# Pooled attention: sums of four tokens made by adding transfers, under a planner that models the tensor clock

## The chip, the cores and the metric

The kernel runs on one core of one Trainium2 chip. The metric is the device time of one execution in microseconds (us); the time of the kernel before is the median of three runs.

## What is computed

```python
# q, k, v: (B=8, H=8, S=576, D=64); w1, w2, w3: (512, 768); w_out: (768, 512)
q_d = q.reshape(B, H, 144, 4, D).mean(axis=3)      # k_d, v_d alike
out_d = sm_attn(q_d, k_d, v_d)                     # softmax attention over 144 pooled tokens
out_up = np.repeat(out_d, 4, axis=2)
mask = np.abs(pos[:, None] - pos[None, :]) < 4     # seven neighbours
out_local = softmax(where(mask, scale * q @ k.T, -1e9)) @ v
x = (out_up + out_local).transpose(0, 2, 1, 3).reshape(B * S, H * D)      # (4608, 512)
h = np.maximum(np.maximum(x @ w1, x @ w2), x @ w3)
return h @ w_out
```

The MLP weights arrive as float64. The means are made as sums; their quarter is in the scale of the scores and in later factors.

## The kernel before

The work is cut into nine blocks, j = 0 to 8. Blocks 0 to 7 hold the first 512 tokens of a batch each, block 8 the last 64 of all eight. Each of the first eight has two halves of four heads, n = 2j and 2j + 1. The engines are TensorE (PE), VectorE (DVE), ScalarE (ACT), GpSimd (POOL) and SyncE (SP), which issues every DMA of this kernel.

*Local attention.* Blocks 0 and 1 are "dense" (`dense`, L1132): `band_load` (L777) brings q and k transposed, `band_scores` (L813) multiplies them on TensorE and takes the softmax of a band (row maxima `mxb`, sums `zb`, the scaling `wlo<-wlo,zb`), `band_values` (L847) multiplies with v. Blocks 2 to 7 work by windows (`scores` L706, `values` L746): products `prod` and sums on VectorE, products `pv` on GpSimd or ScalarE.

*Pooled attention* needs, for each half, the transposed sums `qkT` (128 x 2 x 2 x 144: q and k, two pairs of heads, 128 sums and 16 of the tail), the sums of v as `vd` (128 x 4 x 64) and of v's tail as `vs` (128 x 64). `pooled_scores` (L634) takes maxima `nm`, the exponentials and `pd`, `ptail`; `pooled_values` (L686) gives `od` and `odtail`. The sums come from four places. `tail_pooled` (L611) loads `traw` and `pt` and adds twice by way of `th`. In dense blocks `band_sums` (L801) adds the band's own q and k (by way of tag `q`), and `band_pooled_values` (L878) loads v again and adds it by way of `hv`. In windowed blocks `scores` loads `qt_pool` and `kt_pool` into `hqk` and adds them by way of `qd` and `kd` on GpSimd, and `values` adds the v that it has by way of `hv`.

*MLP.* `turn(j)` (L1168) transposes a block's x and splits it into two float32r parts, `xhi` and `xlo` (`xlo<-t,xhi`, one per 128 columns, four per block). A weight comes in 24 pieces of 512 KB (`weight_piece`, L583); `weight_split` (L572) makes of each a float32 (`hqk`: an absolute value on ScalarE, two TENSOR_SCALAR and two SCALAR_TENSOR_TENSOR, STT below, on VectorE) and its two parts `whi` and `wlo` (or `wo`). `mlp_column` (L912) makes 128 hidden columns with three groups of twelve matmuls, the contraction chunks c = 0 to 3 in order:

```python
ops = [(a[ft][:, i, c], b[c]) for c in range(NCC) for a, b in ((whi, blk["hi"]), (wlo, blk["hi"]), (whi, blk["lo"]))]
```

and `mlp_out` (L929) multiplies with `w_out`. The last two blocks go through `joint_in` (L1047), which shares products between them.

*What sets the order.* Every operation is first recorded (`Recorder`, L150; hence all of them show one line in the trace, L459, after the change L499). `place` (L288) then lays them on five engines by prices (`price`, L244), priorities and a model of the DMA rings (`Rings`, L116), and `emit` (L415) writes them out in that order, one queue per engine, each executed in sequence. Priorities are set with `at(...)`: `FIRST` and `LATE` for the halves of dense blocks, a line in the number of pieces for weights (L1176). TensorE's prices are multiplied by a fixed 1.65 between 11 and 82 us:

```python
if e == "PE" and WARM < t < SLOW:
    c *= COLD
```

Of the kernel before, what the change touches and what calls it, by code (L numbers as in the profile page):

```python
# [21 lines left out]
P = 128  # L22
# [22 lines left out]
WPRIO = (20.0, 60.0, 105.0, 150.0, 160.0, 170.0, 180.0)  # L45
# [62 lines left out]
def pe_kind(o):  # L108
    method, args, _ = o.forms["PE"][0]
    if method == "transpose":  # L110
        return "T" if list(args[1].ap)[0][1] > T32 else "t"
    kind = {F32R: "R", BF16: "B"}.get(args[1].dtype, "M")
    return "P" if kind == "M" and elems(args[0]) in (P, 6) else kind


class Rings:  # L116
# [6 lines left out]
    def issue(self, t, on_chip, outside):  # L123
        src, dst = [[list(d) for d in ap.ap] for ap in (outside, on_chip)]
        run = src.pop()[1] if src[-1][0] == 1 and len(src) > 1 else 1
        rows = int(np.prod([c for _, c in src]))
        k = max(x for x in range(1, 17) if src[0][1] % x == 0 and dst[0][1] % x == 0)
        each = rows // k
        lane = self.count % LANES
        self.count += 1  # L130
        t = max(t, self.lanes[lane])
        while True:
            left = sum(n * min(1.0, (b - max(t, a)) / (b - a)) for a, b, n in self.queue if b > t)
            if left + each <= RING or not left:
# [12 lines left out]
        return t, done, end  # L147


class Recorder:  # L150
# [93 lines left out]
    def price(self, eng, method, args, kw):  # L244
# [7 lines left out]
        if eng == "PE":  # L252
# [11 lines left out]
            return 165.0 if n > P else 125.0, False  # L264
# [15 lines left out]
        if eng == "POOL":  # L280
            if method == "memset":
# [6 lines left out]
    def place(self):  # L288
        ops = self.ops
        for o in ops:  # L290
            o.users, o.left, o.ready, o.eng, o.waits = [], len(o.need), 0.0, None, []
            o.cost = {}
# [15 lines left out]
        rings = Rings()  # L308
        queue = {e: [] for e in ENGINES}
# [24 lines left out]
        while len(out) < len(ops):  # L334
# [34 lines left out]
            if e == "PE" and WARM < t < SLOW:  # L369
                c *= COLD  # L370
# [5 lines left out]
            else:  # L376
# [3 lines left out]
                o.end = t + c + DONE_NS[e]  # L380
            o.stop = free[e]
# [16 lines left out]
            for u in o.users:  # L398
                u.left -= 1
                same = tuple(u.forms) == (e,) and e != "SP"  # L400
# [70 lines left out]
def local_global_attention_maxout_kernel(ctx: ExitStack, tc: tile.TileContext, q, k, v, qt_dense, kt_dense, qt_pool, kt_pool, qkt_tail, v_dense, v_tail, w_in, w_out, ident_d, mask_d, band_d, out):  # L471
# [139 lines left out]
    def tail_pooled(n):  # L611
        j, h0 = n // 2, HH * (n % 2)
        st = state[n]
        qkT = st["qkT"]
        dense_n = n < 2 * NDENSE
        raws = []
        for g, src in enumerate((qkt_tail[j, n % 2], v_tail[j, h0 : h0 + HH])):
            tag = (("traw", "pt") if n != 1 else ("traw", "k"))[g] if dense_n else "traw"
            raw = new([P, FAC * D], tag=tag, bufs=2 if tag == "k" else 1, name=f"traw_{n}_{g}")
            with late(n):  # L620
                sp.dma_start(raw, src if g == 0 else src.rearrange("h r x -> (h r) x"))
            h = new([P, 2 * D], tag="th", name=f"th_{n}_{g}")
# [83 lines left out]
    def scores(n):  # L706
# [7 lines left out]
        for g in range(HH):  # L714
# [10 lines left out]
            if j < B:  # L725
                w, pr = ("q", "k")[g // 2], g % 2
                if g == 0:
                    qkT = st["qkT"] = new([P, 2, 2, SD], tag="qkT", bufs=2, name=f"qkT_{n}")
                raw = new([P, SEG], tag="hqk", bufs=2, name=f"raw{w}_{n}_{pr}")
                sp.dma_start(raw, (qt_pool, kt_pool)[g // 2][j - NDENSE, h0 // 2 + pr])  # L730
                half = new([P, 2 * P], tag=f"{w}d", name=f"h{w}_{n}_{pr}")
                tt(half, raw[:, : 2 * P], raw[:, 2 * P :], ALU.add, ("POOL",))
                tt(qkT[:, g // 2, pr, :P], half[:, :P], half[:, P:], ALU.add)
# [12 lines left out]
    def values(n):  # L746
# [4 lines left out]
        if j < B:  # L751
            hv = new([P, HH, 2 * D], tag="hv", name=f"hv_{n}")
            vd = st["vd"] = new([P, HH, D], tag="vd", bufs=2, name=f"vd_{n}")
        for g in range(HH):
# [11 lines left out]
            if j < B:  # L766
                halves(n, "v", vv[:, 3 * D : 7 * D], hv[:, g])
# [5 lines left out]
        if j < B:  # L773
            tt(vd, hv[:, :, :D], hv[:, :, D:], ALU.add)
# [25 lines left out]

    def band_sums(n, pr, tag):  # L801
        st = state[n]
        if pr == 0:
            st["qkT"] = new([P, 2, 2, SD], tag="qkT", bufs=2, name=f"qkT_{n}")
        qkT, band = st["qkT"], st["band", pr]
        for a, x0 in enumerate((0, SEG + 3)):
            dst3 = band[:, x0 : x0 + SEG].rearrange("p (r f) -> p r f", f=FAC)
            h = new([P, P, 2], tag="q", bufs=2, name=f"hq_{n}_{pr}_{a}")
            o1 = qkT[:, a, pr, :P]
            pair = [("tensor_tensor", (), dict(out=h, in0=dst3[:, :, :2], in1=dst3[:, :, 2:], op=ALU.add)), ("tensor_tensor", (), dict(out=o1, in0=h[:, :, 0], in1=h[:, :, 1], op=ALU.add))]  # L810
            rec.add({"POOL": pair, "DVE": pair})
# [65 lines left out]

    def band_pooled_values(n):  # L878
        j, h0 = n // 2, HH * (n % 2)
        vd = state[n]["vd"] = new([P, HH, D], tag="vd", bufs=2, name=f"vd_{n}")  # L880
        hv = new([P, HH, 2 * D], tag="hv", name=f"hv_{n}")
        for g in range(0, HH, 2):
            vv = new([P, 2, FAC * D], tag="v", bufs=2, name=f"v_{n}_{g}")
            with late(n):
                sp.dma_start(vv, dram(v, (j * H + h0 + g) * S * D, [[FAC * D, P], [S * D, 2], [1, FAC * D]]))
            halves(n, "v", vv, hv[:, g : g + 2])
        tt(vd, hv[:, :, :D], hv[:, :, D:], ALU.add)

# [229 lines left out]
    def attention(n):  # L1118
        j = n // 2
        if n % 2 == 0:  # L1120
            state["blk", j] = {"x": [None] * NCC, "band": {}, "hi": [], "lo": []}
            if j == B:
                state["blk", j]["od"] = odtail.rearrange("p c b t -> p c (b t)")
        scores(n)
        if j < B:
            tail_pooled(n)
# [5 lines left out]
    def dense(j):  # L1132
# [5 lines left out]
        def pooled(n, _):  # L1138
            tail_pooled(n)
            pooled_scores(n)  # L1140
            band_pooled_values(n)
# [66 lines left out]
def lay_out(q, k, v, moe_w1, moe_w2, moe_w3, moe_w_out):  # L1208
    first, rest = slice(0, NDENSE), slice(NDENSE, B)
# [3 lines left out]
    for name, x in zip(("qt_pool", "kt_pool"), pairs):  # L1213
        named[name] = x[rest, :, :, :SEG].reshape(B - NDENSE, H // 2, P, P, FAC).swapaxes(3, 4).reshape(B - NDENSE, H // 2, P, SEG)
    tails = np.stack([x[..., SEG:].reshape(B, 2, 2, P, TAIL, FAC) for x in pairs])
    named["qkt_tail"] = tails.transpose(1, 2, 4, 0, 3, 6, 5).reshape(B, 2, P, FAC * FAC * TAIL)
    named["v_dense"] = v[first].transpose(0, 2, 1, 3).reshape(NDENSE, S, H * D)
    named["v_tail"] = v[:, :, FAC * (SD - T32) :].reshape(B, H, T32, FAC * D)
# [30 lines left out]
```

## Time and profile before

| | |
|---|---|
| median of three runs | 742.05 us (742.05, 742.05, 742.7) |
| the profiled execution: its time and its span | 742.2 us (nothing lies around the span), 11812 instructions |
| TensorE busy | 712.6 us, 96% |
| VectorE busy | 658.4 us, 89% |
| ScalarE busy | 422.8 us, 57% |
| GpSimd busy | 331.9 us, 45% |
| DMA | 92.20 MB, 39.3% of the sixteen engines' span |
| chain that ended last | TensorE 84%, VectorE 7%, DMA 6% |

A profile is of one execution. "Busy" is the time in which an engine had an instruction under way; the ends of matmuls are modelled and neighbours overlap. "Clock" is the share of full speed that TensorE was granted, where 0.50 stands for 1.2 GHz and 1.00 for 2.4 GHz.

### The profile page before, as it was taken

The page shows a single profiled execution, that of the slowest core. Times are in us where ns is not written, and L with a number is a line of the kernel's source. Part 1 is how long each engine was busy: PE and PEld are TensorE (multiplying, and loading weights), DVE is VectorE, ACT ScalarE, POOL GpSimd, SP SyncE. Part 2 cuts the span into 40 slices and gives each one's busy share as a digit, 9 for nine tenths or more (in the row PEclk, how much of TensorE's full clock was granted, in tenths as well). Part 3 has the DMA queues.
Part 4 walks back from the last instruction along what each step waited for, and adds up shares of the span by engine and source line. Part 5 has one row for each costly group of instructions (what it writes and reads, how often), then busy time and mean ns, then how long its engine had stood idle before and what let it go on. Part 6 is the DMA issues. An engine that isn't in the chain of part 4 may idle for free.

```text
span 742.2 us, 11812 instructions
## 1 busy us (share of the span) xinstructions
PE 712.6 (96%) x3820; PEld 566.6 (76%) x3820; DVE 658.4 (89%) x980; ACT 422.8 (57%) x1415; POOL 331.9 (45%) x545
## 2 busy tenths in 40 slices
PE   5877899999999999999999999999999999999996
PEld 3654677878788778777887787878778888888885
DVE  6999998999999998999999999999989999988520
ACT  4776767526484557557473748577395547433221
POOL 0001001038894739585573858788186336321000
PEclk9769999999999999999999999999999999999999
DMA  8954334265555535653454444633342310000012
GB/s 265 332 198 146 93 93 150 89 186 193 167 168 164 154 92 153 185 165 108 150 160 139 127 140 149 181 97 122 93 136 77 105 47 28 1 1 0 1 57 57
DMA packets 51561, 92.20 MB, mean 124 GB/s; under 512 B 5645, under 2 KB 21311, under 8 KB 51499
## 3 DMA queue, kind: packets, MB, share of 16 engines
q1 hardware_dynamic: 51498, 91.45, 39.3%
q8 instruction: 30, 0.49, 0.3%
q14 instruction: 33, 0.26, 0.1%
HBM read 81.99 MB, written 9.44 MB: 123 GB/s over the span
## 4 chain that ended last, share of the span: by engine, by line
PE 84%; DVE 7%; DMA 6%; SPq 1%; issue 1%; ACT 0%; ACTq 0%; DVEq 0%
PE pm L459 71%; PE pa L459 13%; DVE hqk L459 3%; DMA whi<-in_kt_dense_dram 2%; DMA pv<-in_kt_dense_dram 1%; DMA wo<-in_w_in_dram 1%; DMA hh<-in_w_in_dram 1%; DVE wlo_0r L459 1%; PE pq L459 1%; DMA v<-in_v_dram 1%; SPq L459 1%; DMA pv<-in_moe_w_out_dram 1%; DVE t L459 0%; DVE mxb L459 0%; DVE xlo_0r L459 0%
## 5 line engine op out<-in xcount | busy, mean ns | idle before, releaser
L459 PE MATMUL pm<-xhi_0r,whi_0r 128*128 128x512 f32 x552 | 218.3, 395 | 0.0
L459 PE MATMUL pm<-xhi_0r,wlo_0r 128*128 128x512 f32 x552 | 218.2, 395 | 0.0
L459 PE MATMUL pm<-xlo_0r,whi_0r 128*128 128x512 f32 x552 | 216.7, 397 | 0.0
L459 POOL TENSOR_TENSOR pv<-v,sums 128x256 f32<-128x256 f32 x244 | 146.7, 703 | 15.8 <-DMA v<-in_v_dram 6.0
L459 ACT ACTIVATE pv<-v,sums 128x64 f32<-128x64 f32 x536 | 141.5, 414 | 13.9 <-POOL sums L459 6.4
L459 PE MATMUL pm<-wo_0r,hh_0r 128*128 128x512 f32 x576 | 138.3, 393 | 0.5 <-DVE wo_0r L459 0.5
L459 PEld LDWEIGHTS pm<-wo_0r,hh_0r 128*128 128x128 f32 x576 | 106.7, 188 | 23.2 <-DVE wo_0r L459 0.9
L459 PEld LDWEIGHTS pm<-xlo_0r,whi_0r 128*128 128x128 f32 x552 | 103.9, 189 | 23.2 <-issue 1.1
L459 PEld LDWEIGHTS pm<-xhi_0r,wlo_0r 128*128 128x128 f32 x552 | 104.3, 189 | 22.6 <-issue 1.5
L459 PEld LDWEIGHTS pm<-xhi_0r,whi_0r 128*128 128x128 f32 x552 | 104.2, 189 | 21.8 <-issue 0.7
L459 DVE TENSOR_REDUCE sums<-prod 128x28 f32<-128x1792 f32 x56 | 112.6, 2011 | 0.5
L459 DVE TENSOR_TENSOR prod<-k,pq 128x1792 f32<-128x1792 f32 x56 | 112.1, 2002 | 0.4
L459 DVE TENSOR_REDUCE x<-pv 128x256 f32<-128x1792 f32 x44 | 88.3, 2012 | 5.0 <-ACT pv L459 3.3
L459 ACT CAST hh_0r<-pm 128x512 fp32r<-128x512 f32 x48 | 28.2, 588 | 69.7 <-DVE pm L459 69.5
L459 ACT COPY y<-pm 128x512 f32<-128x512 f32 x46 | 26.8, 589 | 53.2 <-PE pm L459 44.0
L459 POOL TENSOR_TENSOR th<-traw 128x128 f32<-128x128 f32 x25 | 11.6, 464 | 73.5 <-DVE vs L459 47.5
L459 DVE TENSOR_TENSOR t<-pm,t 128x512 f32<-128x512 f32 x46 | 31.5, 685 | 9.7 <-PE pm L459 9.7
L459 POOL TENSOR_TENSOR pv<-pv 128x768 f32<-128x768 f32 (+1 forms) x24 | 37.1, 1547 | 0.9
L459 ACT COPY pq<-q 128x256 f32<-128x256 f32 x56 | 22.3, 399 | 23.2 <-DVE prod L459 19.2
L459 ACT COPY t<-pm 128x512 f32<-128x512 f32 x44 | 25.9, 589 | 16.9 <-PE pm L459 16.4
L459 DVE TENSOR_TENSOR pm<-pm,t 128x512 f32<-128x512 f32 x46 | 31.9, 693 | 3.0 <-PE pm L459 1.9
L459 DVE TENSOR_TENSOR hh_0r<-pm,hh_0r 128x512 fp32r<-128x512 f32 x48 | 32.6, 680 | 0.9 <-ACT hh_0r L459 0.7
(321 smaller groups left out, 1096.3 us busy)
## 6 DMA issues: line engine op xcount, KB each, us to landing
k<-in_k_dram SPq DMA_DIRECT2D x55, 320.0 KB
v<-in_v_dram SPq DMA_DIRECT2D x54, 320.0 KB
out_dram<-y SPq DMA_DIRECT2D x36, 256.0 KB
q<-in_q_dram SPq DMA_DIRECT2D x56, 128.0 KB
hqk<-in_qt_pool_dram SPq DMA_DIRECT2D x24, 256.0 KB
hqk<-in_kt_pool_dram SPq DMA_DIRECT2D x24, 256.0 KB
hh<-in_w_in_dram SPq DMA_DIRECT2D x10, 512.0 KB
pv<-in_w_in_dram SPq DMA_DIRECT2D x5, 512.0 KB
```

The source lines that it names most:

```text
L459: getattr(self.engines[o.eng], method)(*map(real, args), **{k: real(x) for k, x in kw.items()})
```

## The change

Each half's sums now come from DMA. The host lays q, k and v out in four parts by the token's place in its group of four (`qk_pool`, `v_pool`). `pooled_sums` has SyncE load the first part, and GpSimd issue three more transfers into the same tile with `accum_op=add`; `vs` is a fifth part of `vd`. The loads and additions of `tail_pooled`, `halves`, `band_sums`, `band_pooled_values` and those in `scores` and `values` are gone. Per half SyncE loads 295 + 164 = 459 KB for it, and GpSimd three times as much, 1376 KB.

The planner changes as well: TensorE's prices follow a model of its clock (`Clock`), small fp32 matmuls cost 118 or 109 ns in place of 165 or 125, and adding transfers have prices of their own (`SOFT`, `Rings.adding`). So the whole order is made anew. The weights' priorities have their old values under a name.

```diff
-WPRIO = (20.0, 60.0, 105.0, 150.0, 160.0, 170.0, 180.0)
+WEIGHTS = (40.59, 1.14)
...
+SOFT = (1100.0, 900.0, 1200.0, 1.3)
-SLOW = 82000.0
+WINDOW = 3413.3
+PHASE = 2200.0
+KEEP = 0.352
+EASY = 0.0
+GUARD = 0.0
-COLD = 1.65
-WARM = 11000.0
+COLD = 1.9
...
+def pe_load(o):
+    work = 0.0
+    for method, args, kw in o.forms["PE"]:
+        passes = 2.0 if method == "transpose" else 1.0 if args[1].dtype in (F32R, BF16) else 4.0
+        work += elems(args[0]) * passes * (list(args[1].ap)[0][1] / P) * (elems(args[1]) / P if method != "transpose" else 1.0)
+    return work / 2.4 / WINDOW
+class Clock:
...
+    def at(self, t):
+        w = int((t - PHASE) // WINDOW)
...
+        return 1.0 if self.use.get(w - 1, 0.0) >= KEEP + GUARD else COLD
+    def spend(self, t, load):
+        w = int((t - PHASE) // WINDOW)
+        self.use[w] = self.use.get(w, 0.0) + load
...
+    def adding(self, t, on_chip):
+        run = elems(on_chip)
+        work = P // 16 * (8.5 + 0.0377 * 4 * run) * SOFT[3]
+        for e in range(16):
+            self.free[e] = max(self.free[e], t + SOFT[1]) + work
+        return max(self.free) + SOFT[2]
...
-            return 165.0 if n > P else 125.0, False
+            return 118.0 if n > P else 109.0, False
...
-            if e == "PE" and WARM < t < SLOW:
-                c *= COLD
+                c *= clock.at(t)
+                clock.spend(t, pe_load(o))
...
-    def tail_pooled(n):
...
+    def pooled_sums(n):
+        j, st = n // 2, state[n]
+        qkT = st["qkT"] = new([P, 2, 2, SD], tag="qkT", bufs=2, name=f"qkT_{n}")
+        vd = st["vd"] = new([P, HH + 1, D], tag="vd", bufs=2, name=f"vd_{n}")
+        st["vs"] = vd[:, HH]
+        for t, src in ((qkT.rearrange("p a b s -> p (a b s)"), qk_pool), (vd.rearrange("p g d -> p (g d)"), v_pool)):
             with late(n):
+                sp.dma_start(t, src[j, n % 2, 0])
+                for f in range(1, FAC):
+                    gps.dma_start(t, src[j, n % 2, f], accum_op=ALU.add)
...
-            if j < B:
-                w, pr = ("q", "k")[g // 2], g % 2
...
-                sp.dma_start(raw, (qt_pool, kt_pool)[g // 2][j - NDENSE, h0 // 2 + pr])
...
-    def band_sums(n, pr, tag):
...
-    def band_pooled_values(n):
...
+    named["qk_pool"] = np.stack([x.reshape(B, 2, 2, P, SD, FAC) for x in pairs]).transpose(1, 2, 6, 4, 0, 3, 5).reshape(B, 2, FAC, P, 4 * SD)
...
+    named["v_pool"] = np.concatenate([vp[:, :, :, :P].reshape(B, 2, FAC, P, HH * D), vt], -1)
```

**How the order moves on VectorE.** The place is the second pair of `xlo` of block 0 (the third and fourth contraction chunk). Before:

```order
L459 TENSOR_REDUCE mxb_191<-pa_236 128x2
L459 TENSOR_REDUCE mxb_191<-pa_240 128x2
...
L459 TENSOR_TENSOR vd_354<-hv_231 128x256
L459 TENSOR_SCALAR hqk_357<-hqk_357 128x512
L459 TENSOR_TENSOR t_753<-x_642,od_504 128x512
L459 TENSOR_TENSOR t_519<-x_707,od_504 128x512
L459 TENSOR_TENSOR wlo_0r<-hqk_376,whi_0r 128x512
L459 TENSOR_TENSOR xlo_0r<-t_753,xhi_0r 128x512
L459 TENSOR_TENSOR xlo_0r<-t_519,xhi_0r 128x512
```

With the change:

```order
L499 TENSOR_SCALAR hqk_307<-hqk_307 128x512 x2
L499 TENSOR_TENSOR wlo_0r<-hqk_323,whi_0r 128x512
L499 SCALAR_TENSOR_TENSOR hqk_307<-hh_0_259,hqk_307 128x512
L499 TENSOR_TENSOR t_764<-x_508,od_643 128x512
L499 TENSOR_TENSOR t_659<-x_596,od_643 128x512
L499 TENSOR_REDUCE mxb_181<-pa_527 128x2
L499 TENSOR_SCALAR hqk_323<-hqk_323 128x512
L499 TENSOR_TENSOR xlo_0r<-t_764,xhi_0r 128x512
L499 TENSOR_TENSOR xlo_0r<-t_659,xhi_0r 128x512
```

The wlo of the row before is the sixth weight piece's in the old order; ten stand ahead of the pair in the new one, and the eleventh has begun. The sums (`vd<-hv` is one) are gone.

**On TensorE**, the first float32r product. Before:

```order
L459 MATMUL pm_161<-ident_154,wlo_0_570 128x128 x4
L459 MATMUL pm_157<-ident_154,wlo_0_570 128x128 x4
L459 MATMUL pq_272<-ident_154,wlo_0_570 6x32 x8
L459 MATMUL pm_164<-xhi_0r,whi_0r 128x512
L459 MATMUL pm_164<-xhi_0r,wlo_0r 128x512
L459 MATMUL pm_164<-xlo_0r,whi_0r 128x512
L459 MATMUL pq_272<-y_323,wo_0_133 64x128
```

With the change:

```order
L499 MATMUL pa_519<-ptt_607,vd_174 64x144 x2
L499 MATMUL pa_515<-ptt_607,vd_174 64x144 x2
L499 MATMUL pa_527<-qkT_211 128x144 x2
L499 MATMUL pa_519<-qkT_211 128x144 x2
L499 MATMUL pa_515<-qkT_211 32x144 x4
L499 MATMUL pm_165<-xhi_0r,whi_0r 128x512
L499 MATMUL pm_165<-xhi_0r,wlo_0r 128x512
L499 MATMUL pm_165<-xlo_0r,whi_0r 128x512
```

The first product now stands behind the last values of the dense block 0, the pooled values of half 0 and the pooled scores of half 1 (`qkT_211`). Ahead of the first product of the third chunk there are 24 of them, 9 before; the pooled scores of half 0 have moved from before the values of the dense block to behind three sets of them.

**On GpSimd**, the first rows. Before:

```order
L459 TENSOR_TENSOR th_212<-traw_179 128x128
L459 TENSOR_TENSOR vs_350<-th_212 128x64
L459 TENSOR_TENSOR qkT_169<-th_212 128x4x16
L459 TENSOR_TENSOR th_212<-pt_181 128x128
L459 TENSOR_TENSOR hv_231<-v_189 128x128
```

With the change (`qkT_172` and `vd_174` are of half 0, `qkT_211` and `vd_215` of half 1):

```order
L499 DMA qkT_172<-in_qk_pool_dram 128x576
L499 DMA vd_174<-in_v_pool_dram 128x320
L499 DMA qkT_172<-in_qk_pool_dram 128x576
L499 DMA qkT_211<-in_qk_pool_dram 128x576
L499 DMA vd_174<-in_v_pool_dram 128x320
L499 DMA vd_215<-in_v_pool_dram 128x320
L499 DMA qkT_172<-in_qk_pool_dram 128x576
L499 DMA qkT_211<-in_qk_pool_dram 128x576
L499 DMA vd_174<-in_v_pool_dram 128x320
L499 DMA vd_215<-in_v_pool_dram 128x320
L499 DMA qkT_211<-in_qk_pool_dram 128x576
L499 DMA vd_215<-in_v_pool_dram 128x320
```

The twelve adding transfers of halves 0 and 1 stand first, the two halves interleaved. Each waits for the one before it into the same tile. In all GpSimd has 96 of them, 72 for the windowed blocks; SyncE's issues fall from 354 rows to 297.

## Rows read from the trace of the kernel before

**Rows 1.** The page: span, and busy time of each engine.
```profile
span 742.2 us, 11812 instructions
PE 712.6 (96%) x3820; PEld 566.6 (76%) x3820; DVE 658.4 (89%) x980; ACT 422.8 (57%) x1415; POOL 331.9 (45%) x545
```
**Rows 2.** Windows: length, busy per engine (count), then clock, DMA share, GB/s.
```profile
0.00:90.00 90.00, 66.58 (x540) 47.54 (x541) 80.87 (x231) 60.05 (x209) 3.86 (x10) 0.83 0.64 213
150.00:600.00 450.00, 450.00 (x2289) 360.38 (x2289) 430.23 (x485) 270.55 (x966) 292.58 (x492) 1.00 0.46 141
27.00:63.20 36.20, 28.26 (x245) 20.20 (x244) 34.24 (x94) 27.10 (x92) 1.34 (x2) 0.74 0.68 235
63.20:90.00 26.80, 20.80 (x170) 14.72 (x170) 26.38 (x67) 18.32 (x59) 1.42 (x3) 0.92 0.31 93
14.00:22.00 8.00, 5.64 (x52) 4.17 (x50) 7.86 (x26) 6.08 (x26) 0.89 (x2) 0.84 1.02 345
16.00:28.00 12.00, 9.64 (x86) 7.60 (x84) 11.43 (x36) 9.81 (x39) 0.89 (x2) 0.64 1.02 373
```
**Rows 3.** Waits of TensorE from 90 us to the end: total us, times, longest.
```profile
PE pm L459 <- DVE wo_0r L459: 0.5, 1, 0.5
```
**Rows 4.** The chain of waits, 0 to 92 us: start, us, what was waited for.
```profile
2.61 4.76 DMA whi<-in_kt_dense_dram
...
23.06 9.60 DMA pv<-in_kt_dense_dram
```
**Rows 5.** VectorE's groups by form, 27.0 to 63.2 us: busy, mean ns.
```profile
L459 DVE SCALAR_TENSOR_TENSOR hqk<-hh,hqk 128x512 uint32<-128x512 uint32 x11 | 7.6, 688 | 0.2
L459 DVE TENSOR_TENSOR wlo_0r<-hqk,whi_0r 128x512 fp32r<-128x512 f32 x6 | 4.1, 683 | 0.0
L459 DVE TENSOR_REDUCE mxb<-pm 128x2 f32<-128x268 f32 x8 | 3.3, 428 | 0.0
...
L459 DVE TENSOR_SCALAR hqk<-hqk 128x512 f32<-128x512 f32 x5 | 2.1, 420 | 0.0
...
L459 DVE TENSOR_TENSOR qkT<-q 128x128 f32<-128x128 f32 x6 | 1.8, 292 | 0.2
L459 DVE TENSOR_TENSOR q<-pv 128x256 f32<-128x256 f32 x4 | 1.7, 418 | 0.6 <-DMA pv<-in_qt_dense_dram 0.6
```
**Rows 6.** Timeline of VectorE: start, us, instruction.
```profile
25.65 1.42 DVE L459 SCALAR_TENSOR_TENSOR hqk<-hh,hqk 128x512 uint32<-128x512 uint32 x2
...
61.99 1.28 DVE L459 TENSOR_TENSOR xlo_0r<-t,xhi_0r 128x512 fp32r<-128x512 f32 x2
```
**Rows 7.** Timeline of TensorE: start, us, instruction.
```profile
50.66 0.79 PE L459 MATMUL pm<-xhi_0r,whi_0r 128*128 128x512 f32 x1
...
58.14 0.40 PE L459 MATMUL pm<-xlo_0r,whi_0r 128*128 128x512 f32 x1
...
80.98 0.63 PE L459 MATMUL pm<-xhi_0r,whi_0r 128*128 128x512 f32 x1
...
82.82 1.80 PE L459 MATMUL pq<-y,wo 128*64 128x128 f32 x14
...
87.98 1.09 PE L459 MATMUL pq<-y,wo 128*64 128x128 f32 x16 [0.46 <-ACT wlo L459]
...
118.12 0.39 PE L459 MATMUL pm<-xhi_0r,wlo_0r 128*128 128x512 f32 x1
...
121.74 0.39 PE L459 MATMUL pm<-xlo_0r,whi_0r 128*128 128x512 f32 x1
```
**Rows 8.** DMA issues of SyncE: count, KB each.
```profile
traw<-in_qkt_tail_dram SPq DMA_DIRECT2D x16, 128.0 KB
v<-in_v_dram SPq DMA_DIRECT2D x8, 256.0 KB
```
**Rows 9.** GpSimd's groups by form, whole span: busy, mean ns, idle before.
```profile
L459 POOL TENSOR_TENSOR hv<-v 128x128 f32<-128x128 f32 x48 | 22.2, 468 | 6.4 <-DMA v<-in_v_dram 6.2
...
L459 POOL TENSOR_TENSOR qd<-hqk 128x256 f32<-128x256 f32 x24 | 18.0, 751 | 21.0 <-DMA hqk<-in_qt_pool_dram 21.0
```

More of the change, by code (lines that the diff above doesn't have):

```diff
@@ L291, in place @@
             o.users, o.left, o.ready, o.eng, o.waits = [], len(o.need), 0.0, None, []
+            o.dma = next(iter(o.forms.values()))[0][0] == "dma_start"
             o.cost = {}
@@ L308, in place @@
         rings = Rings()
+        clock = Clock()
         queue = {e: [] for e in ENGINES}
@@ L380, in place @@
                 o.end = t + c + DONE_NS[e]
+                if o.dma:
+                    o.end = rings.adding(t + c, o.forms[e][0][1][0])
             o.stop = free[e]
@@ L399, in place @@
                 u.left -= 1
-                same = tuple(u.forms) == (e,) and e != "SP"
+                same = tuple(u.forms) == (e,) and e != "SP" and not o.dma
                 u.ready = max(u.ready, free[e] + (0.0 if e == "PE" else 115.0) if same else o.end + u.lag)
@@ L470, in local_global_attention_maxout_kernel @@
 @with_exitstack
-def local_global_attention_maxout_kernel(ctx: ExitStack, tc: tile.TileContext, q, k, v, qt_dense, kt_dense, qt_pool, kt_pool, qkt_tail, v_dense, v_tail, w_in, w_out, ident_d, mask_d, band_d, out):
+def local_global_attention_maxout_kernel(ctx: ExitStack, tc: tile.TileContext, q, k, v, qt_dense, kt_dense, qk_pool, v_dense, v_pool, w_in, w_out, ident_d, mask_d, band_d, out):
     nc = tc.nc
@@ L799, in band_load_v @@
         sp.dma_start(vt[:, 1:], dram(v_dense, (j * S + P - 3) * row + h0 * D, [[row, P], [P * row, FAC - 1], [1, HH * D]]))
-    def band_sums(n, pr, tag):
[L802 to L811, printed above, removed]
     def band_scores(n, pr, tag):
@@ L876, in band_values @@
         copy(xb, px.rearrange("p u (r f) -> p f (u r)", f=FAC))
-    def band_pooled_values(n):
[L879 to L887, printed above, removed]
     def transposes(j, c):
@@ L1123, in attention @@
                 state["blk", j]["od"] = odtail.rearrange("p c b t -> p c (b t)")
+        if j < B:
+            state[n] = {}
+            pooled_sums(n)
         scores(n)
         if j < B:
-            tail_pooled(n)
             pooled_scores(n)
@@ L1150, in dense @@
         scores = {n: [(n, band_scores, pr, tag) for pr in range(2)] for n in ns}
-        sums = {n: [(n, band_sums, pr, tag) for pr in range(2)] for n in ns}
         values = {n: [(n, band_values, pr, tag) for pr in range(2)] for n in ns}
         if j == 0:
-            order = [load[a][0], load[b][0], load[a][1], load[b][1]] + scores[a] + sums[a] + values[a] + scores[b] + sums[b] + values[b] + [(a, pooled, 0), (b, pooled, 0)]
+            order = [load[a][0], load[b][0], load[a][1], load[b][1]] + scores[a] + values[a] + scores[b] + values[b] + [(a, pooled, 0), (b, pooled, 0)]
         else:
-            order = load[a] + scores[a] + sums[a] + values[a] + load[b]
-            order += [scores[b][0], sums[b][0], (a, pooled, 0), values[b][0], scores[b][1], sums[b][1], values[b][1], (b, pooled, 0)]
+            order = load[a] + scores[a] + values[a] + load[b]
+            order += [scores[b][0], (a, pooled, 0), values[b][0], scores[b][1], values[b][1], (b, pooled, 0)]
         for x in order:
@@ L1174, in weights @@
         for x in which:
-            with at(40.59 + state["pieces"] * 1.14):
+            with at(WEIGHTS[0] + state["pieces"] * WEIGHTS[1]):
                 f(x)
@@ L1208, in lay_out @@
 def lay_out(q, k, v, moe_w1, moe_w2, moe_w3, moe_w_out):
-    first, rest = slice(0, NDENSE), slice(NDENSE, B)
+    first = slice(0, NDENSE)
     pairs = [x.reshape(B, H // 2, 2, S, D).transpose(0, 1, 2, 4, 3).reshape(B, H // 2, P, S) for x in (q, k)]
@@ L1212, in lay_out @@
     named["qt_dense"], named["kt_dense"] = (x[first] for x in pairs)
[L1213 to L1216, printed above, removed]
+    named["qk_pool"] = np.stack([x.reshape(B, 2, 2, P, SD, FAC) for x in pairs]).transpose(1, 2, 6, 4, 0, 3, 5).reshape(B, 2, FAC, P, 4 * SD)
     named["v_dense"] = v[first].transpose(0, 2, 1, 3).reshape(NDENSE, S, H * D)
-    named["v_tail"] = v[:, :, FAC * (SD - T32) :].reshape(B, H, T32, FAC * D)
+    vp = v.reshape(B, 2, HH, SD, FAC, D).transpose(0, 1, 4, 3, 2, 5)
+    vt = vp[:, :, :, SD - T32 :].swapaxes(3, 4).reshape(B, 2, FAC, P, D)
+    named["v_pool"] = np.concatenate([vp[:, :, :, :P].reshape(B, 2, FAC, P, HH * D), vt], -1)
     w = np.stack([moe_w1, moe_w2, moe_w3]).reshape(3, NCC, P, NFT, P)
```

45 lines of the change are left out of this document (7 added, 38 removed).

## The prediction

> **What bounds the kernel now.** I read the page first: TensorE is busy 712.6 of 742.2 us and VectorE 658.4, so at most 29.6 us of TensorE idle time can be won [rows 1]. The windows tell where it lies. From 150 to 600 us TensorE is busy all 450.00 us; from 0 to 90 it is busy 66.58, so 23.4 us of the idle time and all of the slow clock that matters (mean 0.83) are in the first 90 us [rows 2]. From 90 us on, the list of waits has one row for TensorE, 0.5 us [rows 3]. So the change can win only in the opening, and anything it does to SyncE, GpSimd or VectorE afterwards can only lose.
>
> In the opening, the chain of waits goes through transfers first: a load of 257.5 KB takes 4.76 us from issue to landing at 2.61 us and 9.60 us at 23.06 [rows 4]. From 47 to 88 us it is VectorE nearly without a gap. The window 27.00 to 63.20 says the same: VectorE busy 34.24 of 36.20 us, TensorE only 28.26, at a mean clock of 0.74 [rows 2]. What VectorE does there is in its groups: splitting of weight pieces (STT, TENSOR_SCALAR, wlo), softmax of the dense blocks, and the sums of four that the change removes [rows 5].
>
> What ends the opening is a **gate**. An MLP column takes its contraction chunks in order; the first two come with the first pair of `xlo`, and the third needs the second pair, which VectorE ends at 63.2 us [rows 6]. TensorE begins its first float32r product at 50.66, the ninth at 58.14, then runs dry until the gate [rows 7]. Behind the gate it still loses: 26.80 − 20.80 = 6.0 us of idle to 90 us, 20.80 × (1 − 0.92) = 1.7 of clock [rows 2], and the 0.5 of rows 3: 8.2 us. After that it is dense.
>
> So the time is: gate, plus what TensorE must still do, plus what is lost behind the gate. Against the profiled execution's own 742.2 us:
> T = 742.2 + (new gate − 63.2) − (products done earlier) + (new loss − 8.2).
> The profiled execution is 0.15 us above the median of 742.05.
>
> **The change part by part.** *When VectorE ends the bits of the first weight piece (t1).* Now its two STT end at 25.65 + 1.42 = 27.0 us [rows 6]. Ahead of it SyncE now issues per half (n = 0 and 1) 459 KB of sums in place of 128 + 128 + 2 × 256 = 768 KB [rows 8]: 618 KB less in all, and in this stretch the engines move 345 GB/s [rows 2], so 1.8 us earlier. Against it stand GpSimd's adding transfers, 1376 KB a half. They share the engines with SyncE's loads: between 16 and 28 us the mean busy share is 1.02 [rows 2], so no byte is free. The first link of each of the four chains (918 KB of the 2753) can start before the first weight piece has landed; at 373 GB/s that is 2.5 us. t1 = 27.0 − 1.8 + 2.5 = 27.7. Bounds: 25.2 with none ahead, 32.6 with all twelve (7.4 us). The Trainium skill, "DMA: Bandwidth & Descriptors", "Issuing engines are not separate DMA queues", says that transfers of any issuing engine run on the same 16 engines and interleave; by it the 2.5 us count, and a free second path would give 25.2 and T 2.5 lower. No run here shows yet which.
>
> *From t1 to the second xlo pair.* Before, 29 groups add to 40.7 us of durations within 36.2 elapsed, because an instruction's end overlaps the next one's start: 0.89 us elapsed per us listed. The changed order puts between the same two points 19 STT (13.1 us), 20 TENSOR_SCALAR of 512 (8.4), 18 subtractions or adds of 512 (10 wlo, 4 t, 4 xlo: 12.3), 9 maxima mxb (3.9) and 10.3 of other steps: 48.0, with durations from rows 5. The sums that are gone from the stretch are worth 7.0 (six q at 0.42, six qkT at 0.29, and 2.7 of hv, vd and th), but four more weight pieces (2 STT, 2 TENSOR_SCALAR and a wlo: 2.9 us each) stand ahead of the gate: 10 are whole there, where 6 were. 48.0 × 0.89 = 42.7, so the gate is at 27.7 + 42.7 = 70.4, 7.2 us later. With t1's bounds: 67.9 to 75.3.
>
> *What TensorE does ahead of it.* In the changed order 24 float32r products stand ahead of the third chunk, 9 before. Dense, 16 of them take 121.74 − 118.12 = 3.62 us [rows 7], 0.227 each; 15 × 0.227 = 3.4 us done earlier. The pooled scores of half 0 move back behind three sets of values. Nothing on TensorE waits there that VectorE doesn't hold anyway (TensorE is idle 7.9 of 36.2 us), so I cost that at nothing; if that cover goes, the eight matmuls of those scores come on top, small ones, under 2 us.
>
> *Behind the gate.* VectorE was busy 26.38 of 26.80 us there [rows 2], and its weight pieces held TensorE. With 4.5 fewer of 18 pieces left (13 us of VectorE's time), I take the 6.0 of idle as gone. What stays is one start at the slow clock: the four products from 80.98 to 82.82 (1.84 us) and the fourteen small matmuls of 1.80 us behind them show it at that level [rows 7]; against 4 × 0.227 and 1.09 us for sixteen of the latter at 87.98 this is 0.93 + 0.85 = 1.8 us. And the 0.5 of rows 3. New loss 2.3; bounds 0.5 and 8.2 (nothing won).
>
> *Adding transfers as such.* The trace has none. Nearest rows: 4.76 us and 9.60 us for 257.5 KB [rows 4]; a link of 295 KB lies near them, nearer the upper end while the share is 1.02. Half 0's base load is issued where the tail's load now is (5.2 us) and lands at about 12. Three links later it is 26 to 41 us; its scores and maxima need some 3 us more, and VectorE reaches nm of half 0 at t1 + 16.3 = 44.0, of half 1 at 55.6. So they are hidden, with 0 to 15 us to spare.
>
> *Steady state.* GpSimd loses qd, kd, hv, qkT, vd and the tails: 18.0 + 17.7 + 22.2 + 22.1 + 9.0 + 21.0 = 110.0 us, and gets 72 issues [rows 9]. In the windowed blocks VectorE and ScalarE keep their work. TensorE is full, so this wins nothing. SyncE loses 57 issues: nothing. The planner's prices (clock, 118 for 165) are no work; they show only in the order, counted above.
>
> Sum: 742.2 + 7.2 − 3.4 + (2.3 − 8.2) = **740.1 us**.
>
> **Rivals.** *A, the forecast:* 737.6 to 745.0 by the bounds of t1; 746.0 if nothing is won behind the gate.
>
> *B, the head shortens outright.* VectorE loses 7.0 us of sums in the stretch and some 9 ahead of it, and the weights are all split some 9 us earlier. If TensorE isn't held by the gate at 70 but has other work, or VectorE reaches it at about 66, with next to no loss behind it: 742.2 + 2.8 − 3.4 − 8.2 = 733.4. For: VectorE bounds the opening. Against: the order has the four extra pieces ahead of the gate.
>
> *C, slower: the sums of half 0 come late.* A chain has three links in a row, and GpSimd waits in its queue ahead of each. Decisive point: (44.0 − 3 − 12) / 3 = 9.7 us a link, hardly over the 9.60 of a plain load at a share of 1.02. Above it VectorE, which takes its orders in sequence, stands at nm of half 0 and every weight piece and both xlo pairs stand behind it. At 12.3 a link: 3 × 2.7 = 8 us, T = 748.1. Beside this: the Trainium skill, "Collectives: The Full Stack", "The bandwidth ceiling: the fold count and why AG ≠ RS ≠ AR", says that an add in a transfer needs two source reads and so halves the rate. By that rule a link would be up to 19.2 us and T far above 750; no run here shows it yet, and that passage is of transfers between cores.
>
> *D, slower later on.* GpSimd is busy 292.58 of 450 us [rows 2]; without the sums some 450 − 292.6 + 110 = 267 us are free. If it stands for every link of two chains side by side, 36 × 4.76 = 171 us fit, but 36 × 9.60 = 346 don't: 79 too many, 6.6 us for each of 12 halves. Two of them reaching TensorE: 753. For: the queue is in order, and products for windowed values stand behind adding transfers. Against: the share is lower there (0.46), and halves are made ahead.
>
> **Chances.** A 0.50, B 0.18, C 0.20, D 0.12. A measurement here tells a change from none at about 0.2% (1.5 us): 740.6 to 743.5 is "the same". Of A 0.27 lies below, 0.16 within, 0.07 above; B is faster; C is above but 0.02, D is above but 0.01. Faster 0.45, same 0.19, slower 0.36. The range 733 to 752 holds A, most of B and of C, and leaves out most of D and the far end of C. A's own range is 738 to 745.
>
> **What would show it.** Right: the second xlo pair ends at 68 to 75 us; ten weight pieces are split by then; the first float32r product is followed by some 24 before TensorE runs dry; from the gate to 100 us TensorE idles under 2 us; from 100 us it has no wait. VectorE has no wait on the adding transfers. Wrong: VectorE idle ahead of nm of half 0 (C); TensorE waits on x or prod after 100 us, with GpSimd in transfers' waits (D); a gate below 67 (B); a first weight piece landing after 28 us, so that t1 was mis-sized.

## The result: 0.6% slower, where 0.3% faster was forecast

The changed kernel takes 746.16 us (median of 745.58, 745.76, 746.57 and 748.68) against 742.17 for the kernel before beside it: ratio 1.006, interval 1.0042 to 1.0078. The forecast was 740.1. The range (733 to 752) holds the time; the direction was wrong.

The page of the changed kernel, for [rows 1]; the queue lines give packets, MB, and the time of the packets as a share of sixteen engines' span:

```profile
span 743.8 us, 11620 instructions
PE 719.7 (97%) x3820; PEld 571.0 (77%) x3820; DVE 638.0 (86%) x918; ACT 427.8 (58%) x1441; POOL 315.6 (42%) x431
q1 hardware_dynamic: 42410, 79.91, 33.8%
q0 software_dynamic: 13824, 22.03, 18.9%
```

VectorE is 20 us less busy and TensorE 7 us more. The profiled execution took 745.76 us by the clock that the runs are timed with: 1.96 us lie around its span. The table ahead of the prediction says that nothing lies around the span of the kernel before; that was read from a span beside other executions' times, and is wrong (below).

The windows, for [rows 2]:

```profile
0.00:90.00 90.00, 72.71 (x476) 52.43 (x477) 67.53 (x173) 56.89 (x194) 23.18 (x29) 0.90 0.93 254
150.00:600.00 450.00, 450.00 (x2281) 361.37 (x2280) 430.28 (x491) 275.79 (x993) 249.90 (x359) 1.00 0.59 150
27.00:63.20 36.20, 28.29 (x199) 20.18 (x198) 32.46 (x76) 26.03 (x89) 8.62 (x11) 0.78 1.00 300
63.20:90.00 26.80, 24.38 (x142) 17.62 (x141) 23.13 (x56) 16.82 (x55) 8.13 (x10) 0.95 0.81 158
16.00:28.00 12.00, 11.22 (x94) 8.60 (x95) 5.69 (x12) 5.50 (x15) 4.75 (x5) 1.00 1.07 325
```

From 150 us on TensorE is as full as before. In the opening the DMA engines are what changed: a share of 1.00 where it was 0.68 (27 to 63 us) and 0.81 where it was 0.31 (63 to 90), and at full share they move 325 GB/s where they moved 373.

The waits of TensorE from 90 us on, for [rows 3], and the chain of waits from 0 to 100 us, for [rows 4]:

```profile
PE pm L499 <- ACT whi_0r L499: 0.4, 1, 0.4
PE pm L499 <- DVE wlo_0r L499: 0.2, 1, 0.2
```

```profile
2.62 4.98 DMA whi<-in_kt_dense_dram
...
13.32 9.74 DMA hh<-in_w_in_dram
...
77.00 7.69 DMA hh<-in_moe_w_out_dram
```

Two weight pieces stood in the old chain as well, with 6.2 to 6.3 us each:

```profile
16.83 6.21 DMA hh<-in_w_in_dram
...
33.54 6.28 DMA wo<-in_w_in_dram
```

In the new chain there is one of the first pieces too, and it takes 9.74 us; a piece of `w_out` has come in at 77, behind the gate. VectorE's 41 us of the old chain have shrunk. The timelines of VectorE and of TensorE, for [rows 6, 7]:

```profile
24.12 1.41 DVE L499 SCALAR_TENSOR_TENSOR hqk<-hh,hqk 128x512 uint32<-128x512 uint32 x2
...
71.67 1.28 DVE L499 TENSOR_TENSOR xlo_0r<-t,xhi_0r 128x512 fp32r<-128x512 f32 x2
```

```profile
41.67 1.97 PE L499 MATMUL pa<-qkT 64*128 64x144 f32 x16
...
58.50 0.80 PE L499 MATMUL pm<-xhi_0r,whi_0r 128*128 128x512 f32 x1 [0.92 <-ACT xhi_0r L499]
...
84.72 0.39 PE L499 MATMUL pm<-xhi_0r,wlo_0r 128*128 128x512 f32 x1
86.82 0.28 PE L499 MATMUL pa<-prod 128*128 128x268 bf16 x1 [1.71 <-ACT wlo L499]
...
88.43 0.63 PE L499 MATMUL pm<-xhi_0r,whi_0r 128*128 128x512 f32 x1
```

So t1 (the end of VectorE's work on the first weight piece's bits) is 25.5 us, the gate (the end of the second pair of `xlo`) 72.95, and behind it TensorE stalls once more for 1.71 us, with a slow clock after it (0.63 us for a product that took 0.39 before). The pooled scores of half 0 (41.67) waited for nothing: the sums were there in time.

### The profile page after: what moved, and what is told of

Same layout as the page of the kernel before. It is cut to its first block, busy times and chain, and to the rows that moved or that the text cites. A ratio compares the mean times of both kernels' runs of the same rounds, so it can differ in the third digit from the quotient of the medians.

```text
span 743.8 us, 11620 instructions
## 1 busy us (share of the span) xinstructions
PE 719.7 (97%) x3820; PEld 571.0 (77%) x3820; DVE 638.0 (86%) x918; ACT 427.8 (58%) x1441; POOL 315.6 (42%) x431
## 3 DMA queue, kind: packets, MB, share of 16 engines
q1 hardware_dynamic: 42410, 79.91, 33.8%
q0 software_dynamic: 13824, 22.03, 18.9%
## 4 chain that ended last, share of the span: by engine, by line
PE 90%; DMA 4%; DVE 3%; ACT 2%; issue 0%; SPq 0%; ACTq 0%
PE pm L499 73%; PE pa L499 14%; PE pq L499 2%; DMA hh<-in_w_in_dram 1%; DVE hqk L499 1%; DMA hh<-in_moe_w_out_dram 1%; ACT wlo L499 1%; DMA whi<-in_kt_dense_dram 1%; DMA whi<-in_qt_dense_dram 1%; DVE wlo_0r L499 1%; DVE t L499 1%; ACT hqk L499 0%; DVE mxb L499 0%; SPq L499 0%; ACT whi_0r L499 0%
## 5 line engine op out<-in xcount | busy, mean ns | idle before, releaser
L499 PE MATMUL pm<-xlo_0r,whi_0r 128*128 128x512 f32 x552 | 219.1, 397 | 0.3 <-DVE xlo_0r L499 0.3
L499 ACT ACTIVATE pv<-v,sums 128x64 f32<-128x64 f32 x564 | 147.6, 413 | 13.0 <-POOL sums L499 6.6
L499 PEld LDWEIGHTS pm<-wo_0r,hh_0r 128*128 128x128 f32 x576 | 107.0, 188 | 23.2 <-issue 0.9
L499 PEld LDWEIGHTS pm<-xlo_0r,whi_0r 128*128 128x128 f32 x552 | 104.4, 189 | 23.2 <-issue 1.3
L499 POOL DMA_DIRECT2D qkT<-in_qk_pool_dram x48 | 44.8, 939 | 128.6 <-DMA qkT<-in_qk_pool_dram 114.0
L499 DVE TENSOR_REDUCE x<-pv 128x256 f32<-128x1792 f32 x43 | 86.4, 2012 | 9.7 <-POOL pv L499 6.5
L499 POOL DMA_DIRECT2D vd<-in_v_pool_dram x48 | 44.8, 940 | 78.9 <-DMA vd<-in_v_pool_dram 73.2
L499 POOL TENSOR_TENSOR pv<-pv 128x768 f32<-128x768 f32 (+1 forms) x26 | 42.5, 1636 | 1.8 <-ACT pq L499 0.6
L499 ACT ACTIVATE pa<-pa,nm 128x144 f32<-128x144 f32 x80 | 28.5, 357 | 16.7 <-DVE nm L499 15.5
```

Source lines behind the costliest of these rows:

```text
L499: getattr(self.engines[o.eng], method)(*map(real, args), **{k: real(x) for k, x in kw.items()})
```

## The experiments

Two theories stood after the result. One (R): an adding transfer (one with `accum_op=add`, "the add" below) holds the DMA engines twice as long per byte, and what it delays are weight pieces. The other (V): the order made anew is worse, whatever makes the sums. Each run below was timed beside the kernel before on its chip, and the ratio is what counts.

### One software transfer, and the add left out

The kernel before plus one transfer of GpSimd's:

```diff
+    extra = sb.tile([P, 2, 12], F32, name="extra")
+    nc.gpsimd.dma_start(extra, mask_d.rearrange("m p x -> p m x"))
     rec.emit()
```

> The kernel before, with one transfer more: GpSimd loads the 12 KB mask a second time, into a tile that nobody reads. The changed kernel's four times lie 1.96 to 1.98 us above their own spans (745.76 against 743.8), the profiled one of the kernel before 0.0. Theory O (outside): any transfer issued by GpSimd costs a fixed 2.0 us around the span, so this kernel takes 744.2 us at a span of 742.2. Rival P (per transfer): the 2 us come from the 96 transfers, 20 ns each, and one costs nothing outside: 742.2. Rival Q: the gap is part of the measurement of another kernel binary and has nothing to do with transfers: any value, not tied to this edit.

It took 741.66 us, ratio 1.0001 (0.9983 to 1.0018). Its profiled execution took 743.04 at a span of 741.3: 1.7 us around the span and no gain or loss. All twelve runs have 1.7 to 2.0 us there, those without any GpSimd transfer too (the planner's part alone, below: 746.42 at 744.6), and so has the kernel before: 1.73 to 1.85 us in each of its 59 executions beside these runs. Theories O and P fall. The profiled execution of the kernel before, with a span of 742.2, therefore took about 744.0 (an estimate from these): some 2 us more than its median. So its profile and the changed kernel's lie 1.6 us apart (743.8 − 742.2), where the medians lie 4.0 apart.

The changed kernel without the add, in the same order on every engine (its pooled sums then hold one part of the four):

```diff
-                    gps.dma_start(t, src[j, n % 2, f], accum_op=ALU.add)
+                    gps.dma_start(t, src[j, n % 2, f])
```

> The changed kernel with accum_op left out: the 96 transfers of GpSimd overwrite in place of adding, so the pooled sums hold the fourth token's part alone; same order, same bytes, same issuing engine. Theory R (two for one): an adding transfer holds the DMA engines twice as long per byte (0.86% of the span per MB on GpSimd's queue against 0.42% on SyncE's), and this holds up weight pieces. Then GpSimd's share falls from 18.9% to about 9.5%, the mean share of 0 to 90 us from 0.93 to about 0.75, the second xlo pair ends 2 to 3 us earlier than 72.95, and the time is 743.5 to 744.5, with the 2.0 us outside still there. Rival S (software issue): GpSimd's transfers are dear because of who issues them; share and time stay: 18.9%, 746. Rival T (order): neither matters, since the order sets the end; share falls and the time stays within 0.5 us of 746.2.

It took 739.12 us, ratio 0.995 (0.9932 to 0.9969): faster than both kernels, 7.0 us below the changed one, more than R asked for. Queues and windows (its own t1 to gate, and gate to 100 us):

```profile
q1 hardware_dynamic: 42410, 79.91, 33.7%
q0 software_dynamic: 6144, 22.03, 9.6%
```

```profile
23.18:69.78 46.60, 36.74 (x278) 26.17 (x277) 42.55 (x102) 32.70 (x107) 10.43 (x17) 0.74 0.82 288
69.78:100.00 30.22, 30.22 (x227) 22.86 (x226) 26.86 (x63) 22.27 (x74) 1.07 (x2) 1.00 0.43 140
```

The same windows of the changed kernel:

```profile
25.53:72.95 47.42, 38.80 (x269) 27.72 (x266) 43.32 (x103) 32.89 (x107) 13.56 (x15) 0.82 1.01 272
72.95:100.00 27.05, 25.34 (x175) 18.66 (x175) 20.97 (x48) 18.91 (x60) 3.89 (x5) 0.94 0.63 159
```

The same 22.03 MB take 18.9% of the engines' time with the add and 9.6% without: 0.86% and 0.44% per MB, where SyncE's queue has 0.42% (33.8 / 79.91). So it is the add that doubles the time, not the issuing engine; S falls, and so does T, as the order is the same and the time is not. An adding transfer is also cut smaller (1.6 KB a packet, 22.03 MB in 13824, against 3.6), but SyncE's packets, 1.9 KB on average, cost 0.42% per MB: size alone does not look like the reason, though no run separates it from the add. With the add gone, t1 comes 2.4 us earlier and the gate 3.2 (23.2 and 69.8), and behind the gate TensorE is busy 30.22 of 30.22 us at full clock. What was late are the weight pieces. SyncE issued the first of them no later with the add than without (12.20 and 12.59 us), but ScalarE, which takes each piece first, waited longer for them. Its waits from 10 to 40 us, changed kernel, then without the add:

```profile
ACT hqk L499 <- DMA hh<-in_w_in_dram: 4.5, 2, 2.9
```

```profile
ACT hqk L499 <- DMA hh<-in_w_in_dram: 2.0, 1, 2.0
```

### Which adds cost

The add was left out for some halves n only, again in an unchanged order:

```diff
-                    gps.dma_start(t, src[j, n % 2, f], accum_op=ALU.add)
+                    gps.dma_start(t, src[j, n % 2, f], **({} if n < 2 else dict(accum_op=ALU.add)))
```

> The changed kernel, the 12 transfers of halves 0 and 1 without the add (their pooled sums hold one token's part), the other 84 adding; same order. All 96 without it gave 739.1 against 746.2 with it. In that run the first float32r product came at 55.58 in place of 58.50 us and the second xlo pair ended at 69.78 in place of 72.95, and TensorE's wait of 1.71 us at 86.82, with a slow clock behind it, was gone. Theory R1 (what adds beside the first weight pieces holds the gate): this kernel has the gate at about 69.8 again and keeps the stall near 85, so 742.5 to 743.5. Rival R2 (the adds of halves 2 and 3 do it all): 745.5 to 746.5. Rival R3 (halves 0 and 1 are all of it): 739 to 740.

> The changed kernel, the 12 transfers of halves 2 and 3 without the add, the other 84 adding; same order. Theory R1 with its second part: the adds of these halves, issued from 55 to 88 us, hold up the weight piece of w_out that landed at 84.69 after 7.69 us; without them TensorE's stall near 86.8 and the slow clock behind it go (1.7 + about 1.7 us), the gate stays near 73: 742 to 743.5. Rival R2: 739 to 740. Rival R3: 745.5 to 746.5.

> The changed kernel, the 72 transfers of halves 4 to 15 without the add, the 24 of the dense halves adding; same order. From 150 us on TensorE has no wait in the changed kernel, so in every theory of the opening these adds cost nothing: 745.5 to 746.5, with GpSimd's queue at about 12% of the engines' time. Rival (steady state costs, through something the waits don't show): 739 to 744.

| add left out for | time | ratio (interval) | second xlo pair ends |
|---|---|---|---|
| none | 746.16 | 1.006 (1.0042 to 1.0078) | 72.95 |
| halves 4 to 15 | 745.05 | 1.0044 (1.0028 to 1.006) | 73.56 |
| halves 2 and 3 | 742.50 | 1.0009 (0.9999 to 1.0019) | 72.29 |
| halves 0 and 1 | 740.65 | 0.998 (0.9971 to 0.9989) | 69.43 |
| all | 739.12 | 0.995 (0.9932 to 0.9969) | 69.78 |

Without the add on halves 0 and 1 the gate came 3.5 us earlier, as R1 said, and the time fell by 0.8%, more than R1 said (742.5 to 743.5): the stall at 86.8 us went as well, though halves 2 and 3 still add. Without it on halves 2 and 3 the gate hardly moved and that stall went, with the slow clock behind it: 0.5%, as R1 said. TensorE from 85 to 100 us, changed kernel, then without the add on halves 0 and 1, then on 2 and 3:

```profile
85.00:100.00 15.00, 13.29 (x107) 9.93 (x108) 11.75 (x26) 11.20 (x34) 0.94 (x1) 0.89 0.51 135
85.00:100.00 15.00, 15.00 (x136) 11.83 (x137) 12.72 (x28) 11.13 (x38) 0.00 (x0) 1.00 0.33 119
85.00:100.00 15.00, 15.00 (x145) 11.61 (x141) 12.95 (x28) 11.81 (x35) 0.00 (x0) 1.00 0.39 143
```

So there are two places, the gate and the stall behind it, and either of the two edits removes the stall; that is why 0.8 and 0.5 add to more than the 1.1 of all. In the first of the two runs the piece of `w_out` was taken up 5.3 us after its issue (73.52 to 78.78), against 7.69: the last adding transfer of a `qkT` stood 4.4 us ahead of it there (69.11), and 2.3 in the changed kernel (74.75 and 77.00). R2 falls, and R3 too: its number for the first run was near (739 to 740), but by it the second run would have won nothing. The 72 transfers of the windowed halves cost 0.16%, within the intervals of nothing, as a full TensorE lets one expect. That run's gate is the latest of all, and beside it stands something that no run isolates: one pair of `t` ahead of it took 2.87 us, and 2.00 in the changed kernel, each while a GpSimd addition of 1.6 us was under way, but 1.28 without any add, where that addition was over.

VectorE's second xlo pair in these two runs, from its timeline (halves 0 and 1 without the add; then 2 and 3):

```profile
68.15 1.28 DVE L499 TENSOR_TENSOR xlo_0r<-t,xhi_0r 128x512 fp32r<-128x512 f32 x2
```

```profile
71.01 1.28 DVE L499 TENSOR_TENSOR xlo_0r<-t,xhi_0r 128x512 fp32r<-128x512 f32 x2
```

### The planner's part

The kernel before with the new clock and prices, and the changed kernel with the old ones:

```diff
-            if e == "PE" and WARM < t < SLOW:
-                c *= COLD
+            if e == "PE":
+                c *= clock.at(t)
+                clock.spend(t, pe_load(o))
...
-            return 165.0 if n > P else 125.0, False
+            return 118.0 if n > P else 109.0, False
```

> The kernel before with the planner's part of the change alone: the clock that follows use, and the prices 118 and 109 for small matmuls; sums on the engines as before. Theory U (the sums' transfers cost the time): this one is within 2 us of 742.2 either way and the transfers are to blame for the 4 us. Rival V (the order costs it): the new clock makes a worse order, first float32r product late, gate late: 744 or more. A gain of over 2 us (740 or less) would say that the planner's part is good by itself and the sums cost more than the 4 us seen.

> The changed kernel with the planner's old prices (factor 1.65 between 11 and 82 us; 165 and 125 for small matmuls): the sums by adding transfers alone. Theory U: 746 or more, 2.0 of it outside the span, with the DMA share of 0 to 90 us at 0.9 as in the changed kernel. Rival V: 744 or less, with the gate back near 63 to 68 us, since the order was at fault. If both parts cost, 746 to 750.

> The kernel with adding transfers under the planner's old prices (748.5), all 96 transfers without the add. If the add's price is of the chip and not of one order, this one gains about as much as the other pair (7.0): 740.5 to 743. If it lies in how the changed order happens to place weight pieces, the gain is under 3 us: 746 or more. Beside it: if this one is 741 or more where the changed order gives 739.1, the planner's new prices are worth some 2 us here, while under the engine sums they cost 3.9 (746.4).

The planner's part alone: 746.42 us, ratio 1.0049 (1.0033 to 1.0066). V holds there in the time, though not in its reason: the gate came early (58.88 + 1.29 = 60.2 us), but TensorE ran dry later, 4.1 us for block 1's first pooled probabilities (`dtail`) and 2.6 for a weight piece (`whi`). Its window from 100 to 150 us and its waits in it:

```profile
100.00:150.00 50.00, 41.66 (x283) 30.62 (x283) 43.75 (x97) 32.47 (x99) 6.62 (x12) 0.90 0.37 112
```

```profile
PE pa L483 <- DVE dtail L483: 4.1, 1, 4.1
PE pm L483 <- ACT whi_0r L483: 2.6, 1, 2.6
```

The sums alone, under the old prices: 748.5 us, 1.0086 (1.0067 to 1.0105). Without the add: 745.58, 1.0055 (1.0041 to 1.0068), so the add costs 0.3% in that order and 1.1% in the changed one; the expected 740.5 to 743 was missed. In that order the gate hardly moves with the add (72.16 and 71.49 us). VectorE is busy there for 30.68 of the 32 us from 40 to 72 with the add and 28.90 without, so that its own work is the likely holder; no run shows it. So what the add costs depends on the order, and each part of the change is a loss by itself.

### The sums on GpSimd

Three versions load all parts plainly and let GpSimd add them, for halves 0 and 1, 0 to 3, or all. The parts use the buffers of windowed k and v:

```diff
-                    gps.dma_start(t, src[j, n % 2, f], accum_op=ALU.add)
+                    part = new([P, (4 * SD, (HH + 1) * D)[g]], tag="kv"[g], bufs=2, name=f"part_{n}_{g}_{f}")
+                    sp.dma_start(part, src[j, n % 2, f])
+                    gps.tensor_tensor(out=t, in0=t, in1=part, op=ALU.add)
```

A fourth is the kernel before with its dense sums on GpSimd alone (`engines = ("POOL",)` in the dense sums).

> The changed kernel, with the sums of halves 0 and 1 made in another way: SyncE loads all four parts (plain, into the buffers that windowed k and v use later), and GpSimd, which is nearly idle there, adds them; halves 2 to 15 by adding transfers. Without the add on these halves the time was 740.65, 0.998 of before, and wrong in its sums. Theory R1 (it is the add in the transfer, not the bytes, that costs): about 741, 0.997 to 1.000 of before, and right. Rival W (the planner's order, made anew for this, moves the time by as much as the add did): anywhere from 738 to 746. Rival X (GpSimd's adds hold up VectorE where both read the same memory): 744 or more.

> As v_pool01, for halves 0 to 3. With no add in any transfer the time was 739.1, 0.995 of before. Theory R1: 739 to 741. Against it stands that the parts of halves 2 and 3 take the buffers of the first windowed k and v, so the first windowed block's loads come later; by that 741 to 744. Rival W as before.

> As v_pool03, for all sixteen halves: no adding transfer at all. Steady state hides GpSimd's 82 us of sums (110 before). Theory: as v_pool03 or 1 us less (halves 4 to 15 without the add gave 745.05 beside 746.16); if the parts in k and v buffers hold windowed blocks up, TensorE shows waits after 150 us and the time is 745 or more.

> The kernel before, the dense halves' sums allowed on GpSimd alone (before, the planner chose VectorE or GpSimd). If VectorE's sums in the opening are worth their 16 us of time there, this gains as the plain transfers did: 739 to 741. If GpSimd's longer adds (0.46 to 0.75 us in place of 0.29 to 0.42) bring the pooled scores late, 743 to 747.

They took 744.55 (1.0042, 1.0025 to 1.0059), 758.5, 784.5 and 762.7 us. None beats the kernel before, and R1's forecasts for the first three (741 or less) were all missed; for the first, W's wide range holds. X does not show: VectorE's STT take 686 ns in it, as in the changed kernel (20 to 100 us). In the first the gate came at 60.45 us, twelve earlier than in the changed kernel, and the gain was lost behind it (this profile is of an execution of 742.44 us, 2 us under the median):

```profile
60.00:100.00 40.00, 39.68 (x279) 29.61 (x277) 37.86 (x84) 28.25 (x91) 5.80 (x7) 1.00 0.51 123
100.00:150.00 50.00, 42.66 (x284) 30.98 (x281) 42.89 (x89) 32.35 (x96) 11.29 (x12) 0.90 0.70 173
```

TensorE had the first block's work sooner and then stood 7.3 us between 100 and 150 us, most of it for block 1's pooled probabilities (`pd`, 2.5) and a weight piece (`whi`, 3.2), as under the planner's part alone: a gate isn't the bound by itself, only the first of several. The second lost far more than the 741 to 744 that the expectation against it gave, and its reason, a late first windowed block, does not show: TensorE is busy throughout from 150 to 720 us, and the loss is from 100 to 150, 10.2 us of idle at a mean clock of 0.73. The third loses there too and again behind 600 us, where TensorE waits 15.6 us on `x`:

```profile
100.00:150.00 50.00, 39.79 (x246) 29.38 (x245) 42.02 (x94) 32.28 (x104) 6.55 (x7) 0.73 0.59 155
100.00:150.00 50.00, 38.07 (x250) 27.49 (x249) 44.06 (x96) 31.57 (x103) 7.96 (x6) 0.80 0.45 149
600.00:720.00 120.00, 100.29 (x446) 81.29 (x446) 113.49 (x146) 62.05 (x183) 51.07 (x63) 0.91 0.16 49
```

The fourth lies outside everything expected: its gate is early too (59.64 + 1.28 = 60.9 us), and TensorE stands even between 150 and 600 us (441.86 of 450.00 us busy). Why these three lose so much stays open.

## Why the prediction was wrong, step by step

- *The base.* "Profiled execution 0.15 us above the median": wrong. The span of 742.2 was compared with times, and 1.7 to 2.0 us lie between them in every run here, before and after. The sum of 740.1 was a span; as a time it is about 742.0, no change. This is 2 us of the miss of 6.1; 0.4 is the changed kernel's median over its profiled execution; 3.7 is in the span (743.8 against 740.1).
- *t1, 27.7 us forecast, 25.5 measured.* The 1.8 us for fewer loads was too small: SyncE issued the first weight pieces at 12.20 us in place of 16.44, and without the add t1 is 23.2, so that 3.8 were won (27.0 to 23.2), with the bytes of GpSimd's transfers already in it. (A slip of units is in the 1.8: 768 KB was counted by 1024 bytes and 459 by 1000; put right it is 1.9.) The 2.5 us for the first adding transfers is what the add cost (25.5 against 23.2), but by luck: the 2.5 was for their bytes, and what shows is twice the engine time for the same bytes.
- *From t1 to the gate, 42.7 forecast, 47.4 measured.* VectorE's list was sized well: 48.0 us, and the groups of this stretch add to 48.9. The factor of 0.89 was too low. It was taken from a stretch that was itself 34.24 of 36.20 us busy, so the 42.7 stood for about 40.4 us of work and 2.3 of waits; measured are 43.3 and 4.1. The waits are on TensorE's scores (mxb 1.7, nm 0.8) and smaller ones; without the add they are the same (46.60 − 42.55). Together: gate 72.95 in place of 70.4, in the bounds.
- *Products ahead of the gate: right.* The 24 stood there, and five of the third chunk's that need only `xhi`. Before, two such stood there as well, so 18 and not 15 were won: 4.1 us (18 × 0.227).
- *Behind the gate, 2.3 us forecast.* By the balance 743.8 = 742.2 + 9.75 − 4.1 + (L − 8.2), L is 4.15; the rows give 1.71 of idle to 100 us, 1.5 of slow clock (25.34 × 0.06) and 0.6 of later waits, 3.8. The step that failed here is "I take the 6.0 of idle as gone": it was gone with plain transfers (30.22 of 30.22 us, L = 0.7 by the same balance), and a stall was back where both the halves 0 and 1 and the halves 2 and 3 add.
- *Adding transfers: the step that cost the sign.* I costed them by the bytes and at nothing beyond t1, asking only if the sums came late. They did not: C's place was wrong, VectorE never stood at nm for a transfer, and that its 748.1 lies near the measured time is luck. But C's premise, that an add makes a transfer slower, held: 0.86 against 0.44% of the span per MB. The Trainium skill, "Collectives: The Full Stack", "The bandwidth ceiling: the fold count and why AG ≠ RS ≠ AR", says of transfers between cores that an add needs two source reads and so halves the rate. The trace agrees with the half, within one core; the second read it does not show. The victims were other transfers: the first weight pieces, and one of `w_out` at 77 us that took 7.69 us. Without the add the same order takes 739.12 us in place of 746.16. I had looked at who waits for the new transfer, not at who shares its engines.
- *Steady state: right.* GpSimd stands for its adds (114.0 us on qkT, 73.2 on vd over the run) and TensorE never does; D fell.
- *A and B.* Without the add the chip lies between the two: the gate of A (69.78, A said 70.4) and nearly the loss of B (0.7, B said none). Its span of 737.2 is 2.9 us under A's 740.1 and 3.8 over B's 733.4, so A is the nearer of the two.
- *The signs.* All but one of those named for being right came true: the gate at 68 to 75 us, ten pieces split by then, 24 products, 1.71 us of idle from the gate to 100 us, no wait of VectorE on an adding transfer (TensorE waits 0.6 us after 100 us, where none was forecast). None of them looked at the base, at the clock behind the stall or at the other transfers, and so they could hold while the direction was wrong.

## What to carry to other kernels

A transfer that adds into SBUF is not a free adder: here it took twice the engines' time of a plain one, and in a stretch where the DMA engines were already full it delayed the weight pieces beside it, so that the loss showed at unrelated waits. Cost a new transfer by who shares the engines with it, and leave the add out in a throw-away kernel to see the price. And compare a span with spans: a run's time has a part around it.

## What the runs showed of the chip

- Adding transfers: 0.86% of the sixteen engines' span per MB against 0.44% for the same transfers without the add, 13824 packets against 6144. From issue to landing 288 KB took 5.3 us (median) against 3.8.
- GpSimd's own time to issue one rises with the add, 939 ns against 555. The groups of the changed kernel, then of the one without the add:

```profile
L499 POOL DMA_DIRECT2D qkT<-in_qk_pool_dram x48 | 44.8, 939 | 128.6 <-DMA qkT<-in_qk_pool_dram 114.0 <-PE pa L499 13.3 <-issue 1.3
```

```profile
L499 POOL DMA_DIRECT2D qkT<-in_qk_pool_dram x48 | 26.6, 555 | 122.7 <-DMA qkT<-in_qk_pool_dram 121.6 <-issue 0.9
```

- Plain transfers issued by GpSimd cost the engines what SyncE's do (0.44 and 0.42% per MB).
